# Bucket features of an LSH attention on one 64-row block a head instead of four 32-row blocks, with score steps of two PSUM banks

## The chip, the cores and the metric

The kernel runs on one core of a Trainium2 chip. The metric is the device time of one execution in microseconds. A run of several executions gives a median with the lowest and the highest; beside it one execution is recorded by the hardware profiler, and all views of the profile are of that one.

## What is computed

The reference is an attention with locality-sensitive buckets, followed by a gated MLP. Cut to what matters here:

```
q_bucket = bits of (q @ proj > 0)          # 6 bits a row
k_bucket = bits of (k @ proj > 0)
mask   = q_bucket == k_bucket
scores = where(mask, q @ k.T / sqrt(D), -1e9)
attn   = exp(scores - max) / (sum + 1e-9)
x      = attn @ v                          # 4 batches, 8 heads, 768 rows, head size 64
h      = gelu(x @ w_in)                    # then split into u and v
out    = x + (u * (w_sg @ norm(v) + b_sg)) @ w_out
```

All values are float32. The kernel gets the precision with split operands: each matrix is held as a high and a low part, and a product is a sum of three matmuls (high x high, low x high, high x low).

## The kernel before, in words

The kernel has an attention stage and then an MLP stage. The change edits the attention stage.

**Head pairs.** The 32 heads are taken as 16 pairs (`NPAIR`). The two heads of a pair lie one above the other: head 0 on rows (partitions) 0 to 63, head 1 on rows 64 to 127. `parts` transposes q and k on TensorE (L476) and splits them into a high part (L480, ScalarE) and a low part (L483, VectorE). A score matmul then reads 64 rows, and the two heads' matmuls stand beside each other in the array.

**Bucket features.** The mask is not applied afterwards but added inside the score matmul. `features` projects q and k with a signed copy of `proj` (L498) and turns the signs into feature rows (L501): 12 rows a block, six bits each with both signs, and one row in front of them (`MROW` = 0) which holds, on the q side, the shift (the negated maximum of the row) and ones on the k side. So one matmul over 13 rows adds both a huge negative number where the buckets differ and the shift. `block(b)` is the slice of these 13 rows: it starts at row `b * BL` and is `1 + 2 * NB` = 13 rows long. In the kernel before, `BL` is 32: there are four blocks, at rows 0, 32, 64 and 96, two with the same content for each head (head j has blocks 2j and 2j + 1).

**A score step.** There are 96 steps, six for each pair. `maxima(g + AHEAD)` runs `largest` for one tile of 128 query rows, five steps ahead, and `weigh` handles two tiles of 128 keys (`two`) against 384 queries.

- `largest` makes approximate scores with the features (L520) and the high parts (L523), for two halves `kh` of the keys and two heads `j`: four results of 128x384, each in a PSUM bank of its own. VectorE reduces each to its row maximum (L531). Group 0 issues all four 13-row matmuls and then the two 64-row matmuls of half 0; group 1 issues the two of half 1.
- After three tiles, `shift` combines the maxima (L543, L544), lays them out over the blocks with an identity matmul (L550), and ScalarE copies one row for each block into the features of q (L556, four copies).
- `weigh` makes the exact scores of both key tiles: group 0 issues all four 13-row matmuls (L574), then the three passes of the first key tile (L579, two heads each); group 1 issues the three passes of the second. ScalarE takes the exponentials (L586). `product` multiplies them with v (L592; eight matmuls of 128 rows and 64 columns), and the exponentials are added up for the denominators (L601) by the engine that `ADDS` names for the key tile: GpSimd for all five.
- `finish` sums over the partitions with matmuls (L617) and divides.

**What sets the order.** The order of all instructions is written out ahead by `Plan.order`. Every group of instructions is added with an engine, an estimated cost, a priority, and the buffers that it reads and writes. The planner simulates the engines and takes, for each engine, the group that can start first, and among those that can start then the one with the lowest priority number; a group with a better priority that could start within `SOON` times the cost is waited for. Step g has priority 2g for `weigh` (+ 0.01 for its second group), 2g + `S0P` for its `largest`, 2g + `AVP` for the product; `PREP`, `SHIFTP`, `FINP`, `WSTEP` and `WP` are the offsets of the preparation of a pair, the shift, the finish and the splitting of the MLP's weights. `form` marks groups of another tile shape, for which the planner adds 0.09. PSUM has eight banks: one holds the product (`NAV` = 1), the other seven are given out by `ps_tile` to whatever group asks; a group starts only when all of its banks are free. Group 0 of `weigh` and group 0 of `largest` ask for four each, since the features of both halves are written there.

Of the kernel before, what the change touches and what calls it, by code (L numbers as in the profile page):

```python
# [15 lines left out]
ALU = mybir.AluOpType  # L16
# [4 lines left out]

MLP = {"xl": "POOL", "gm": "DVE", "gl": "POOL", "wg": 398.29, "wo": 46.93, "x": 568.79}

AVP = 3.77
NAV = 1
S0P = 0.84
AHEAD = 5
PREP, SHIFTP, FINP, WSTEP, WP = -0.26, 2.36, 2.39, 13, 13.23
LOADS = "SP"
ADDS = ["POOL", "POOL", "POOL", "POOL", "POOL"]  # L30


class Plan:
# [3 lines left out]


    WAIT = 0.18
    SOON = 0.32  # L40
    TICK, WARM = 3.413, 0.49
    TURN_PE = 0.09
    LANES = 8
# [58 lines left out]
    def order(self):  # L102
# [32 lines left out]
        while len(out) < len(G):  # L135
# [10 lines left out]
            def early(n):  # L146
                e = G[n]["e"]
                return not wants[n] or e not in first or first[e] == n
# [5 lines left out]
            g = G[n]  # L154
            soon = [m for m in ready[e] if early(m) and max(when(m), since(m)) <= t0 + self.SOON * g["c"] and (G[m]["p"], m) < (g["p"], n)]
            if soon:
# [62 lines left out]
def kernel(  # L219
# [16 lines left out]
    nc = tc.nc  # L236

    B, H, S, D = q.shape
    P = 128
    NT = S // P  # L240
    HT = NT // 2
    SH = S // 2
# [6 lines left out]
    NB = proj.shape[1]  # L249
# [4 lines left out]
    EMPTY = 2.0 ** 32  # L254
# [20 lines left out]

    BL, MROW = 32, 0
    pr = const.tile([P, NB], F32, name="pr")
    for j in range(2):  # L280
        nc.scalar.dma_start(pr[j * D:(j + 1) * D], proj)
# [3 lines left out]
    for s in range(2):  # L285
        pv = pw[:, s, :].rearrange("p (b c) -> p b c", c=BL)
        for j in range(2):
            for r in range(2):
                c0 = 1 + NB * r
                nc.vector.tensor_scalar_mul(pv[j * D:(j + 1) * D, 2 * j:2 * j + 2, c0:c0 + NB],  # L290
                                            pr[j * D:(j + 1) * D].unsqueeze(1).to_broadcast([D, 2, NB]),
                                            1.0 if r == s else -1.0)
    pwh = const.tile([P, 2, P], F32R, name="pwh")
    pwl = const.tile([P, 2, P], F32R, name="pwl")
    nc.scalar.copy(pwh, pw)
# [7 lines left out]
    for s in range(2):  # L303
        for r in range(2):
            c0 = 1 + NB * r
# [60 lines left out]
    PE, DVE, ACT, POOL, SP = "PE", "DVE", "ACT", "POOL", "SP"  # L366
    xs = [[dram.tile([P, S], F32, name=f"xs_{b}_{hp}") for hp in range(NP)] for b in range(B)]

    plan = Plan()
# [45 lines left out]
    if True:  # L415
# [27 lines left out]
        def block(b):  # L443
            return slice(b * BL, b * BL + 1 + 2 * NB)

        def row(j):
            return slice(j * D, (j + 1) * D)
# [59 lines left out]
        def largest(st, t, prio):  # L507

            hf, i = divmod(t, HT)
            if i == 0:  # L510
                st.mx = late.ring([P, 2, HT, 2], F32, "mx", 3)
            mx, qs = st.mx, slice(t * P, (t + 1) * P)
            sc = [[ps_tile() for j in range(2)] for kh in range(2)]

            def mm(kh):
                if kh == 0:
                    for h in range(2):
                        for j in range(2):
                            b = block(2 * j + h)
                            nc.tensor.matmul(sc[h][j]()[:, :SH], st.ft[0]()[b, qs], st.ft[1]()[b, h * SH:(h + 1) * SH],  # L520
                                             start=True, stop=False)
                for j in range(2):
                    nc.tensor.matmul(sc[kh][j]()[:, :SH], st.hi[0]()[row(j), qs], st.hi[1]()[row(j), kh * SH:(kh + 1) * SH],  # L523
                                     start=False, stop=True)

            for kh in range(2):
                plan.add(PE, (0.36, 0.18)[kh], prio + 0.01 * kh, lambda kh=kh: mm(kh),
                         [(st.hi[0], hf), (st.hi[1], kh)] + ([(st.ft[0], hf), st.ft[1]] if kh == 0 else []),
                         sc[kh] + (sc[1] if kh == 0 else []), form="row")
                for j in range(2):  # L530
                    plan.add(DVE, 0.56, prio, lambda j=j, kh=kh: nc.vector.tensor_reduce(  # L531
                        mx()[:, kh, i, j:j + 1], sc[kh][j]()[:, :SH], axis=AX.X, op=ALU.max, negate=True),
                        [sc[kh][j]], [(mx, (kh, j, i))])

        def shift(st, hf, prio):

            mx, m, tp = st.mx, plan.buf("m", len(msts), lambda i: msts[i % len(msts)]), ps_tile()
            V = nc.vector

            def twice():  # L540
                return mx()[:, 0].rearrange("p i j -> p (i j)").unsqueeze(2).to_broadcast([P, 2 * HT, 2])

            plan.add(DVE, 0.16, prio, lambda: V.tensor_tensor(mx()[:, 0], mx()[:, 0], mx()[:, 1], op=ALU.min), [mx], [mx], port=True)  # L543
            plan.add(DVE, 0.16, prio, lambda: V.scalar_tensor_tensor(  # L544
                m()[:, :, MROW::BL].rearrange("p i (j a) -> p (i j) a", a=2), twice(), EMPTY, twice(), op0=ALU.is_lt, op1=ALU.mult),
                     [mx], [m], port=True)

            def spread():
                for i in range(HT):
                    nc.tensor.matmul(tp()[:, i * P:(i + 1) * P], m()[:, i, :], identr, start=True, stop=True)  # L550

            plan.add(PE, 0.35, prio, spread, [m], [tp])
            ft, cs = st.ft[0], slice(hf * SH, (hf + 1) * SH)
            for b in range(4):
                r = b * BL + MROW
                plan.add(ACT, 0.47, prio, lambda r=r: nc.scalar.copy(ft()[r:r + 1, cs], tp()[r:r + 1, :SH]), [tp], [(ft, hf)])  # L556

        def weigh(st, hf, k0, prio):

            cs, two = slice(hf * SH, (hf + 1) * SH), (k0, k0 + 1)  # L560
            if k0 == 0:
                st.av = ps_t.ring([P, 512], F32, "av", NAV)
                st.sum = [late.ring([P, SH], F32, "sum", 4) for _ in range(2)]
            av, sums = st.av, st.sum
            sc, p = [[ps_tile() for j in range(2)] for _ in two], [[p_tile() for j in range(2)] for _ in two]
            (qh, kh), (ql, kl), (qf, kf) = st.hi, st.lo, st.ft

            def mm(i):
                if i == 0:

                    for a, kt in enumerate(two):
                        for j in range(2):
                            b = block(2 * j + a)
                            nc.tensor.matmul(sc[a][j]()[:, :SH], kf()[b, kt * P:(kt + 1) * P], qf()[b, cs],  # L574
                                             start=True, stop=False)
                ks = slice(two[i] * P, (two[i] + 1) * P)
                for n, (x, y) in enumerate(((kh, qh), (kl, qh), (kh, ql))):
                    for j in range(2):
                        nc.tensor.matmul(sc[i][j]()[:, :SH], x()[row(j), ks], y()[row(j), cs], start=False, stop=(n == 2))  # L579

            for i, kt in enumerate(two):
                plan.add(PE, (0.72, 0.53)[i], prio + 0.01 * i, lambda i=i: mm(i),
                         [(x, hf) for x in (qh, ql)] + [(x, kt // HT) for x in (kh, kl)] + ([(qf, hf), kf] if i == 0 else []),
                         sc[i] + (sc[1] if i == 0 else []), form="row")
                for j in range(2):
                    plan.add(ACT, 0.5, prio, lambda i=i, j=j: nc.scalar.activation(p[i][j]()[:, :SH], sc[i][j]()[:, :SH], AF.Exp),  # L586
                             [sc[i][j]], [p[i][j]])

            def product():
                for i, kt in enumerate(two):  # L590
                    for j in range(2):
                        nc.tensor.matmul(av()[row(j), :SH + 1], st.v()[:, j, kt, :], p[i][j](), start=(kt == 0), stop=(kt == NT - 1))  # L592

            plan.add(PE, 1.48, prio + AVP, product, p[0] + p[1] + [st.v], [av], form="col")
            for i, kt in enumerate(two):
                if kt == 0:
                    continue
                e = ADDS[kt - 1]
                for j in range(2):
                    def add(j=j, i=i, first=p[0][j] if kt == 1 else sums[j]):  # L600
                        (nc.gpsimd if e == POOL else nc.vector).tensor_add(sums[j](), first()[:, :SH], p[i][j]()[:, :SH])  # L601

                    plan.add(e, 1.01 if e == POOL else 0.55, prio + 0.6, add, [p[i][j]] + ([p[0][j]] if kt == 1 else []),
                             [sums[j]], port=True)
# [51 lines left out]
        def maxima(i):  # L656
            n, t = divmod(i, NT)
            if n >= NPAIR:
                return
            p0 = 2 * (i - AHEAD) + S0P  # L660
            largest(sts[n], t, p0)
# [8 lines left out]
        for n in range(NPAIR):  # L670
            for c in range(NT):
                if c == 0:
                    prepare(n + 1)
                hf, k0, g = c // HT, 2 * (c % HT), NT * n + c
# [196 lines left out]
    for b in range(B):  # L871
        p = 500 + 1000 * b
        h = hidden(b, xx, p)
# [40 lines left out]
```

## Time and profile before

| | us |
|---|---|
| median of 3 runs | 870.92 |
| lowest, highest | 868.95, 871.54 |
| the profiled execution | 871.28 |
| its span in the trace | 869.5 |
| the attention's score steps, first to last score matmul | 27.2 to 511.2 |

In the profile PE is TensorE, PEld its weight loads, DVE VectorE, ACT ScalarE, POOL GpSimd and SP the engine that issues the transfers. A row of a group names the line, the engine, the operation, what it writes and reads, the shapes as partitions x elements, and the count; then come the busy time in us and the mean length of one in ns, and then the idle time of the engine just ahead of the group's instructions with what ended it. In a row of the timeline the first number is the start, the second the length of the merged piece, and L12 is line 12 of the kernel. Matmuls are pipelined, so the length of one is longer than the distance to the next, and the distance between starts says what a matmul costs when others follow. `g` is one of the seven shared PSUM tiles, `fq` and `fk` are the features, `hq`, `hk` the high parts, `lq`, `lk` the low parts, `p` the exponentials and `av` the product with v.

### The profile page before, as it was taken

The page shows a single profiled execution, that of the slowest core. Times are in us where ns is not written, and L with a number is a line of the kernel's source. Part 1 is how long each engine was busy: PE and PEld are TensorE (multiplying, and loading weights), DVE is VectorE, ACT ScalarE, POOL GpSimd, SP SyncE. Part 2 cuts the span into 40 slices and gives each one's busy share as a digit, 9 for nine tenths or more (in the row PEclk, how much of TensorE's full clock was granted, in tenths as well). Part 3 has the DMA queues.
Part 4 walks back from the last instruction along what each step waited for, and adds up shares of the span by engine and source line. Part 5 has one row for each costly group of instructions (what it writes and reads, how often), then busy time and mean ns, then how long its engine had stood idle before and what let it go on. Part 6 is the DMA issues. An engine that isn't in the chain of part 4 may idle for free.

```text
span 869.5 us, 15645 instructions
## 1 busy us (share of the span) xinstructions
PE 837.3 (96%) x5480; PEld 600.6 (69%) x5480; DVE 572.3 (66%) x1241; ACT 447.4 (51%) x990; POOL 443.9 (51%) x470
## 2 busy tenths in 40 slices
PE   7999999999999999999999979879889999999998
PEld 5655565565565555566656537879788989988996
DVE  7957876777776787687777515988972419515830
ACT  2556666666656656666666754542433225423511
POOL 0567768677767766867777793134111501510030
PEclk9889999999999999999999998979989999999999
DMA  5121321232132132133221123330013240122003
GB/s 139 43 56 50 95 79 53 79 96 65 59 87 74 50 95 67 49 96 93 58 61 53 58 68 111 136 95 27 25 37 124 70 145 1 37 73 74 1 1 121
DMA packets 100590, 60.86 MB, mean 70 GB/s; under 512 B 65696, under 2 KB 92320, under 8 KB 100512
## 3 DMA queue, kind: packets, MB, share of 16 engines
q1 hardware_dynamic: 99200, 56.85, 23.3%
q10 hardware_dynamic: 1312, 3.02, 1.0%
q8 instruction: 43, 0.70, 0.4%
q14 instruction: 35, 0.29, 0.1%
HBM read 47.06 MB, written 12.68 MB: 69 GB/s over the span
## 4 chain that ended last, share of the span: by engine, by line
PE 83%; DVE 8%; DMA 5%; issue 1%; ACT 1%; SPq 1%; POOL 0%; DVEq 0%; ACTq 0%
PE av L592 15%; PE g L579 13%; PE ps_vs L831 11%; PE ps_o L857 8%; PE g L520 6%; PE ps_h L813 6%; PE g L523 6%; PE ps_h L784 4%; PE g L498 4%; PE g L574 4%; PE g L476 3%; PE g L550 2%; PE g L617 2%; PE ps_o L862 1%; DMA rs<-r 1%
## 5 line engine op out<-in xcount | busy, mean ns | idle before, releaser
L601 POOL TENSOR_TENSOR sum<-sum,p 128x384 f32<-128x384 f32 x256 | 255.0, 1030 | 62.4 <-ACT p L586 62.4
L531 DVE TENSOR_REDUCE mx<-g 128x1 f32<-128x384 f32 x384 | 187.0, 549 | 95.7 <-PE g L523 95.6
L586 ACT ACTIVATE p<-g 128x384 f32<-128x384 f32 x384 | 157.6, 494 | 77.5 <-PE g L579 77.4
L592 PE MATMUL av<-p,v 128*64 128x385 f32 x768 | 146.5, 503 | 0.0
L592 PEld LDWEIGHTS av<-p,v 128*64 128x64 f32 x768 | 46.9, 137 | 52.5 <-issue 49.9
L601 POOL TENSOR_TENSOR sum<-p,p 128x384 f32<-128x384 f32 x64 | 63.6, 1015 | 33.2 <-ACT p L586 31.5
L579 PE MATMUL g<-hq,hk 64*128 64x384 f32 x384 | 76.0, 392 | 0.0
L769 DVE SCALAR_TENSOR_TENSOR h<-h,ps_h 128x384 f32<-128x384 f32 (+1 forms) x56 | 33.2, 605 | 64.8 <-ACT h L768 64.4
L794 POOL TENSOR_TENSOR mv<-mv,epsr 128x1 f32<-128x1 f32 x24 | 13.2, 551 | 111.8 <-DVE mv L793 106.6
L556 ACT CAST fq<-g 1x384 fp32r<-1x384 f32 x128 | 60.2, 470 | 13.5 <-PE g L550 12.3
L831 PE MATMUL ps_vs<-wgh,zh 128*128 128x384 f32 x192 | 65.4, 341 | 0.1
L857 PE MATMUL ps_o<-woh,gs 128*128 128x512 f32 x192 | 65.5, 402 | 0.0
L579 PE MATMUL g<-lq,hk 64*128 64x384 f32 x384 | 65.4, 336 | 0.0
L579 PE MATMUL g<-hq,lk 64*128 64x384 f32 x384 | 65.3, 336 | 0.0
L831 PE MATMUL ps_vs<-wgl,zh 128*128 128x384 f32 x192 | 64.9, 338 | 0.0
L831 PE MATMUL ps_vs<-wgh,zl 128*128 128x384 f32 x192 | 64.8, 338 | 0.0
L842 POOL TENSOR_TENSOR gs<-gt,gs 128x384 fp32r<-128x384 f32 x32 | 32.5, 1018 | 60.4 <-ACT gs L839 60.4
L639 POOL TENSOR_TENSOR xt<-xt,e 128x384 f32<-128x384 f32 x32 | 32.5, 1015 | 59.6 <-ACT e L637 49.9
L520 PE MATMUL g<-fk,fq 13*128 13x384 f32 x384 | 61.6, 444 | 0.3
L523 PE MATMUL g<-hk,hq 64*128 64x384 f32 x384 | 60.3, 393 | 0.0
L520 PEld LDWEIGHTS g<-fk,fq 13*128 13x128 f32 x384 | 34.4, 184 | 27.9 <-issue 13.9
L813 PE MATMUL ps_h<-xh,wih 128*128 128x384 f32 x128 | 45.2, 353 | 8.5 <-DVE y L773 7.9
(126 smaller groups left out, 1674.1 us busy)
## 6 DMA issues: line engine op xcount, KB each, us to landing
q<-in_q_dram SPq DMA_DIRECT2D x32, 192.0 KB, 3.0
k<-in_k_dram SPq DMA_DIRECT2D x32, 192.0 KB, 3.4
v<-in_v_dram SPq DMA_DIRECT2D x16, 384.0 KB, 3.4
rs<-r SPq DMA_DIRECT2D x64, 96.0 KB, 2.8
xs<-xt SPq DMA_DIRECT2D x32, 192.0 KB, 2.0
x<-xs SPq DMA_DIRECT2D x16, 384.0 KB, 3.2
rx<-xs SPq DMA_DIRECT2D x96, 64.0 KB, 2.0
out_dram<-ob SPq DMA_DIRECT2D x24, 256.0 KB, 2.1
```

Of the source, the lines that this page charges most:

```text
L498: nc.tensor.matmul(fp()[:, :SH], w[:, s, :], x()[:, cs], start=(i == 0), stop=(i == 2))
L520: nc.tensor.matmul(sc[h][j]()[:, :SH], st.ft[0]()[b, qs], st.ft[1]()[b, h * SH:(h + 1) * SH], start=True, stop=False)
L523: nc.tensor.matmul(sc[kh][j]()[:, :SH], st.hi[0]()[row(j), qs], st.hi[1]()[row(j), kh * SH:(kh + 1) * SH], start=False, stop=True)
L531: plan.add(DVE, 0.56, prio, lambda j=j, kh=kh: nc.vector.tensor_reduce(mx()[:, kh, i, j:j + 1], sc[kh][j]()[:, :SH], axis=AX.X, op=ALU.max ...
L556: plan.add(ACT, 0.47, prio, lambda r=r: nc.scalar.copy(ft()[r:r + 1, cs], tp()[r:r + 1, :SH]), [tp], [(ft, hf)])
L579: nc.tensor.matmul(sc[i][j]()[:, :SH], x()[row(j), ks], y()[row(j), cs], start=False, stop=(n == 2))
L586: plan.add(ACT, 0.5, prio, lambda i=i, j=j: nc.scalar.activation(p[i][j]()[:, :SH], sc[i][j]()[:, :SH], AF.Exp), [sc[i][j]], [p[i][j]])
L592: nc.tensor.matmul(av()[row(j), :SH + 1], st.v()[:, j, kt, :], p[i][j](), start=(kt == 0), stop=(kt == NT - 1))
L601: (nc.gpsimd if e == POOL else nc.vector).tensor_add(sums[j](), first()[:, :SH], p[i][j]()[:, :SH])
L813: nc.tensor.matmul(ps()[:, :SH], w[:, c, fs], x()[:, cs], start=(c == 0 and n == 0), stop=(c == NC - 1 and n == 2))
L831: nc.tensor.matmul(vp(), z()[:, t, fs], w()[:, t, cs], start=(t == 0 and n == 0), stop=(t == NT - 1 and n == 2))
L857: nc.tensor.matmul(po(), a()[:, ts_], w()[:, f, :], start=(f == 0 and n == 0), stop=False)
```

## The change

`BL` goes from 32 to 64, so there is one block of 13 feature rows for each head, at rows 0 and 64. The blocks' 13-row slice itself, `block(b)`, is as before. `largest` and `weigh` are written as two groups each that ask for two banks: each group of `largest` issues the two 13-row matmuls of its half and then the two 64-row ones; each group of `weigh` issues the three passes of its key tile and then the two 13-row matmuls. `shift` writes two rows instead of four and ScalarE copies two. The planner's costs follow, the priorities' offsets get other values, and the addition for the fourth key tile goes from GpSimd to VectorE.

```diff
-AVP = 3.77
+AVP = 1.5
 NAV = 1
-S0P = 0.84
+S0P = 1.0
 AHEAD = 5
-PREP, SHIFTP, FINP, WSTEP, WP = -0.26, 2.36, 2.39, 13, 13.23
+PREP, SHIFTP, FINP, WSTEP, WP = -1, 2, 2.7, 12, 8
 LOADS = "SP"
-ADDS = ["POOL", "POOL", "POOL", "POOL", "POOL"]
+ADDS = ["POOL", "POOL", "DVE", "POOL", "POOL"]
...
-    SOON = 0.32
+    SOON = 0.2
...
-    BL, MROW = 32, 0
+    BL, MROW = 64, 0
...
-                nc.vector.tensor_scalar_mul(pv[j * D:(j + 1) * D, 2 * j:2 * j + 2, c0:c0 + NB],
-                                            pr[j * D:(j + 1) * D].unsqueeze(1).to_broadcast([D, 2, NB]),
-                                            1.0 if r == s else -1.0)
+                nc.vector.tensor_scalar_mul(pv[j * D:(j + 1) * D, j, c0:c0 + NB], pr[j * D:(j + 1) * D], 1.0 if r == s else -1.0)
...
             def mm(kh):
-                if kh == 0:
-                    for h in range(2):
-                        for j in range(2):
-                            b = block(2 * j + h)
-                            nc.tensor.matmul(sc[h][j]()[:, :SH], st.ft[0]()[b, qs], st.ft[1]()[b, h * SH:(h + 1) * SH],
-                                             start=True, stop=False)
-                for j in range(2):
-                    nc.tensor.matmul(sc[kh][j]()[:, :SH], st.hi[0]()[row(j), qs], st.hi[1]()[row(j), kh * SH:(kh + 1) * SH],
-                                     start=False, stop=True)
+                for n, x in enumerate((st.ft, st.hi)):
+                    for j in range(2):
+                        r = (block, row)[n](j)
+                        nc.tensor.matmul(sc[kh][j]()[:, :SH], x[0]()[r, qs], x[1]()[r, kh * SH:(kh + 1) * SH],
+                                         start=(n == 0), stop=(n == 1))
 
             for kh in range(2):
-                plan.add(PE, (0.36, 0.18)[kh], prio + 0.01 * kh, lambda kh=kh: mm(kh),
-                         [(st.hi[0], hf), (st.hi[1], kh)] + ([(st.ft[0], hf), st.ft[1]] if kh == 0 else []),
-                         sc[kh] + (sc[1] if kh == 0 else []), form="row")
+                plan.add(PE, 0.36, prio + 0.01 * kh, lambda kh=kh: mm(kh),
+                         [(st.hi[0], hf), (st.hi[1], kh), (st.ft[0], hf), (st.ft[1], kh)], sc[kh], form="row")
...
-                m()[:, :, MROW::BL].rearrange("p i (j a) -> p (i j) a", a=2), twice(), EMPTY, twice(), op0=ALU.is_lt, op1=ALU.mult),
+                m()[:, :, MROW::BL], mx()[:, 0], EMPTY, mx()[:, 0], op0=ALU.is_lt, op1=ALU.mult),
...
-            for b in range(4):
+            for b in range(2):
...
             def mm(i):
-                if i == 0:
-
-                    for a, kt in enumerate(two):
-                        for j in range(2):
-                            b = block(2 * j + a)
-                            nc.tensor.matmul(sc[a][j]()[:, :SH], kf()[b, kt * P:(kt + 1) * P], qf()[b, cs],
-                                             start=True, stop=False)
                 ks = slice(two[i] * P, (two[i] + 1) * P)
-                for n, (x, y) in enumerate(((kh, qh), (kl, qh), (kh, ql))):
+                for n, (x, y) in enumerate(((kh, qh), (kl, qh), (kh, ql), (kf, qf))):
                     for j in range(2):
-                        nc.tensor.matmul(sc[i][j]()[:, :SH], x()[row(j), ks], y()[row(j), cs], start=False, stop=(n == 2))
+                        r = block(j) if n == 3 else row(j)
+                        nc.tensor.matmul(sc[i][j]()[:, :SH], x()[r, ks], y()[r, cs], start=(n == 0), stop=(n == 3))
 
             for i, kt in enumerate(two):
-                plan.add(PE, (0.72, 0.53)[i], prio + 0.01 * i, lambda i=i: mm(i),
-                         [(x, hf) for x in (qh, ql)] + [(x, kt // HT) for x in (kh, kl)] + ([(qf, hf), kf] if i == 0 else []),
-                         sc[i] + (sc[1] if i == 0 else []), form="row")
+                plan.add(PE, 0.71, prio + 0.01 * i, lambda i=i: mm(i),
+                         [(x, hf) for x in (qh, ql, qf)] + [(x, kt // HT) for x in (kh, kl, kf)], sc[i], form="row")
```

More of the change, by code (lines that the diff above doesn't have):

```diff
@@ L538, in shift @@
             V = nc.vector
-            def twice():
-                return mx()[:, 0].rearrange("p i j -> p (i j)").unsqueeze(2).to_broadcast([P, 2 * HT, 2])
             plan.add(DVE, 0.16, prio, lambda: V.tensor_tensor(mx()[:, 0], mx()[:, 0], mx()[:, 1], op=ALU.min), [mx], [mx], port=True)
             plan.add(DVE, 0.16, prio, lambda: V.scalar_tensor_tensor(
-                m()[:, :, MROW::BL].rearrange("p i (j a) -> p (i j) a", a=2), twice(), EMPTY, twice(), op0=ALU.is_lt, op1=ALU.mult),
+                m()[:, :, MROW::BL], mx()[:, 0], EMPTY, mx()[:, 0], op0=ALU.is_lt, op1=ALU.mult),
                      [mx], [m], port=True)
```

## The prediction

> **What bounds the kernel now.** I read the page's busy shares first, then its slices with the granted clock, then the busy time of the engines in the attention stage (from the first to the last score matmul), and then TensorE's timeline, step by step.
>
> ```profile
> PE   837.3 (96%) x5480; PEld 600.6 (69%) x5480; DVE 572.3 (66%) x1241; ACT 447.4 (51%) x990; POOL 443.9 (51%) x470
> ...
> PE   7999999999999999999999979879889999999998
> ...
> PEclk9889999999999999999999998979989999999999
> ...
> 27.20:511.20 484.00, 480.07 (x3699) 284.29 (x3695) 349.19 (x739) 309.26 (x732) 350.42 (x357) 0.99 0.26 69
> ```
>
> The last row is the attention stage; its columns after the length are the busy times of PE, PEld, DVE, ACT and POOL, the granted clock, and DMA. PE works 480 of 484 us at a granted clock of 0.99, while DVE and POOL have some 134 us free each. The change edits this stage alone. The stage has 96 score steps (16 head pairs of six), so one takes 484 / 96 = 5.04 us, and the kernel's time follows PE's time per step. What lies outside the stage runs the same instructions before and after; I leave it as it is.
>
> Busy time says nothing about what a matmul costs when they overlap. For that I take the starts of the next view: one whole step of the timeline without side work, from one `weigh` to the next (columns: start, length, engine, line).
>
> ```profile
> 256.09 0.45 PE L574 MATMUL g<-fq,fk 13*128 13x384 f32 x4
> 256.47 0.45 PE L579 MATMUL g<-hq,hk 64*128 64x384 f32 x2
> 256.75 0.34 PE L579 MATMUL g<-hq,lk 64*128 64x384 f32 x2
> 256.93 0.34 PE L579 MATMUL g<-lq,hk 64*128 64x384 f32 x2
> 257.11 0.34 PE L579 MATMUL g<-hq,hk 64*128 64x384 f32 x2
> 257.29 0.34 PE L579 MATMUL g<-hq,lk 64*128 64x384 f32 x2
> 257.46 0.34 PE L579 MATMUL g<-lq,hk 64*128 64x384 f32 x2
> 257.74 0.61 PE L520 MATMUL g<-fk,fq 13*128 13x384 f32 x4
> 258.28 0.61 PE L523 MATMUL g<-hk,hq 64*128 64x384 f32 x4
> 258.82 1.51 PE L592 MATMUL av<-p,v 128*64 128x385 f32 x8
> 260.26 0.44 PE L574 MATMUL g<-fq,fk 13*128 13x384 f32 x4
> ```
>
> I call a set of matmuls that run side by side a slot, and a change of form a place where the next slot has another tile shape. Three prices come out of the starts.
>
> - A slot followed by its own kind: from 256.75 to 257.46 there are four, 0.71 / 4 = 0.178 us each. A slot is two 64-row matmuls here. The four 13-row matmuls of L574 are also one slot: together they last 0.45 us, about as long as one pair.
> - The last slot before a change: 257.74 - 257.46 = 0.28, so 0.10 more.
> - The first slot after a change: 256.75 - 256.47 = 0.28, again 0.10 more.
>
> A change of form thus costs 0.20 us, half on each side of it. The lone slot of L574, with a change on both sides, should then take 0.178 + 0.20 = 0.38; it takes 256.47 - 256.09 = 0.38. The same can be seen over the whole run in the mean lengths of the groups:
>
> ```profile
> L579 PE MATMUL g<-hq,hk 64*128 64x384 f32 x384 | 76.0, 392 | 0.0
> L579 PE MATMUL g<-lq,hk 64*128 64x384 f32 x384 | 65.4, 336 | 0.0
> L520 PE MATMUL g<-fk,fq 13*128 13x384 f32 x384 | 61.6, 444 | 0.3
> L574 PE MATMUL g<-fq,fk 13*128 13x384 f32 x384 | 43.9, 442 | 0.6 <-DVE mx L531 0.6
> L523 PE MATMUL g<-hk,hq 64*128 64x384 f32 x384 | 60.3, 393 | 0.0
> ```
>
> Matmuls that never stand first after a change last 336 ns (lq,hk). The 13-row ones, which always do, last 442 to 444, 0.106 more. Those that do half of the time (hq,hk, and L523) lie in between, at 392 and 393. So the price holds for all 384, and it is paid between 13-row and 64-row tiles as between any others.
>
> One more thing is in L520: it has as many matmuls as L574 but 61.6 us of busy time against 43.9. In the step above its four took 0.61 us instead of 0.45: the last of the four starts late, since the step asks for four free PSUM banks at once. That wait is 17.7 / 96 = 0.18 us a step.
>
> Sum of the score part of the step as it is: 10 slots (1 + 6 in `weigh`, 1 + 2 in `largest`) x 0.178 = 1.78; changes: in, three inside, out; the outer two count half, so 4 x 0.20 = 0.80; the bank wait 0.16 here. That is 2.74, and the timeline has 258.82 - 256.09 = 2.73. The model closes.
>
> **The change part by part.** *Slots.* With one block a head, only the two heads of one key tile go side by side, not two heads by two key tiles. `weigh` goes from 7 slots to 8, `largest` from 3 to 4: 2 x 0.178 = +0.36 us a step.
>
> *Changes of form.* The slice that the matmuls read is still 1 + 2 x 6 = 13 rows, so I take their tile to stay the 32-row one, now at rows 0 and 64. Each `weigh` half becomes three 64-row slots and one 13-row slot; each `largest` half one 13-row and one 64-row slot. With all four halves in a row (S 64 rows, F 13 rows): SSSF SSSF FS FS. That has six changes inside against three now (FSSSSSS FSS). With the P·V product L592 between the two `weigh` halves, as the planner may well place it now that the halves are separate and AVP is 1.5, the change from F to S there is swallowed by the two that the product has in any case, and the first `weigh` half joins the last `largest` half as S to S: two more changes instead of three. Strict alternation of the halves (SSSF FS SSSF FS) leaves one more. I expect the first two orders in about equal numbers, since side work (transposes, projections) decides in each step whether the product is ready: 2.5 x 0.20 = +0.50 us a step.
>
> The Trainium skill, "TensorEngine Tiling (Array Packing)", section Key Properties, says that changing the tiling mode, not just the tile, drains TensorE; this speaks against the change. The trace agrees on the 0.10 us before a change (257.46 to 257.74), but shows as much again behind it (256.47 to 256.75), which a drain alone does not name. By the drain alone the added changes would come to 2.5 x 0.10 x 96 = 24 us instead of 48; the rows decide for 48.
>
> *Banks.* Two banks a step instead of four, of seven: the late fourth matmul should go, -0.18 us a step. What remains late next is PE itself, so the gain is real; if the wait only moves, it is lost.
>
> *Other engines.* The two rows of the shift in place of four take 64 copies off ACT, and one addition in five goes from POOL to DVE (the last two rows are from the view of waits: who waited for whom, us in total, times, longest):
>
> ```profile
> L556 ACT CAST fq<-g 1x384 fp32r<-1x384 f32 x128 | 60.2, 470 | 13.5 <-PE g L550 12.3
> L601 POOL TENSOR_TENSOR sum<-sum,p 128x384 f32<-128x384 f32 x256 | 255.0, 1030 | 62.4 <-ACT p L586 62.4
> L531 DVE TENSOR_REDUCE mx<-g 128x1 f32<-128x384 f32 x384 | 187.0, 549 | 95.7 <-PE g L523 95.6
> PE g L617 <- POOL sum L601: 5.4, 2, 5.0
> PE g L617 <- ACT p L586: 2.7, 3, 1.1
> ```
>
> ACT loses 64 x 0.47 = 30 us of 309, POOL 64 x 1.03 = 66 of 350, neither of which PE waits for except the 8 us at L617 (the sums), of which up to 5 may go. DVE gains 64 additions. It does none of this shape now; between its reduction of a 128x384 tile (0.549) and POOL's addition (1.03) that is 35 to 66 us, and I take 35, the same engine and size. It lies beside DVE's 135 us of idle time, and the stage gets longer. Queued behind a DVE addition are the reductions that free the banks of `largest`; if every addition held up PE by its length, 35 us would come on top, but with two banks a step there are three spare ones, so I count nothing. The weight jobs and other planner numbers only move work within queues that are not full; no transfer is added or removed, and SP's and POOL's queues issue the same. Zero for these.
>
> Sum: 0.36 + 0.50 - 0.18 = +0.68 us a step, x 96 = +65 us. The profiled execution took 871.28 us (span 869.5), 0.4 over the median of 870.92. That gives 871.3 + 65 = 936 us.
>
> **The rivals.** *The 13-row matmuls take the 64-row form.* If the two blocks at rows 0 and 64 run in the form of the score passes, no change is left inside the step: 0.36 - 3 x 0.20 - 0.18 = -0.42 us a step, -41 us, 830 us: faster. It decides at the first S to F of a step, which would then be 0.178 instead of 0.28. DVE would have 349 + 35 = 384 us in 443, so the gain could be had. For it: the 64-row spacing of the blocks, and that the row positions are the same as those of the passes. Against it: the 13-row matmuls in the trace of before stand at rows 0 and 64 too, together with 32 and 96, and pay the full price against 64-row ones.
>
> *The order alternates.* One more change only: 0.36 + 0.20 - 0.18 = 0.38 a step, 36 us, 908 us; with the 5 us of L617, 902. For it: each half is now its own group of two banks. Against it: priorities put both `weigh` halves ahead of `largest` (2g against 2g + 1).
>
> *The bank wait stays* while the halves stand in a row: 0.36 + 0.60 = 0.96 a step, 92 us, 963 us. For it: the seven banks are the same, and `weigh` and `largest` of a step ask for eight. Against it: they no longer ask for four at once, and consumers get more time per step.
>
> **How the numbers follow.** The forecast (two or three more changes, wait gone: 926 to 946 us) gets 0.62; alternating order 0.12; bank wait 0.12; the 64-row form 0.11; 0.03 is left for effects that cancel nearly. The range must hold 0.8: from 902 to 962 it takes in the first three (0.86) and leaves out the 830. About 0.3% is what a measurement of this kernel tells from no change (the runs shown span 868.95 to 871.54). Faster by more than that is the 64-row form, 0.11; within it 0.02; slower the rest, 0.87.
>
> **What would show it.** The 13-row matmuls stay 768 in all, but stand in the timeline as slots of two (three slots of L579 and one of two 13-row matmuls in each `weigh` half) in place of fours. Their mean length shows the form: near 0.34 us if they run as the score passes do, 0.40 to 0.44 if they change form; and in the latter case the mean of the 64-row group behind them (hq,hk) stays near 0.39 and that of L523's rises towards 0.44. A step should take some 5.7 us in place of 5.04, with PE busy nearly all of the stage and the granted clock unchanged, and the late start inside the 13-row slots of `largest` should be gone. The order of the halves shows which count of changes holds. The prediction is wrong if a 64-row slot follows a 13-row one after 0.18 us, or if PE is seen waiting for DVE or ACT inside the steps.

## The result, and the profile after

The change makes the kernel slower: 949.41 us median of four runs (944.45 to 952.64) against 870.51 of four, a ratio of 1.0903 (95% interval 1.0851 to 1.0955). The profiled execution took 944.45 us, its span is 942.7, so 73.2 us more than the span of before. The prediction was 936 us, with 902 to 962.

From the page of the kernel after, the rows that answer to the first fence of the prediction. The last row is the busy time of the engines over its attention stage, here from the first `weigh` to the MLP's first matmul.

```profile
PE 916.1 (97%) x5480; PEld 615.7 (65%) x5480; DVE 620.5 (66%) x1369; ACT 419.5 (45%) x926; POOL 316.7 (34%) x342
...
PEclk8999999998999999999998999998999999999999
...
28.00:596.20 568.20, 565.67 (x3717) 304.96 (x3717) 394.66 (x868) 285.49 (x676) 232.05 (x239) 0.98 0.22 60
```

The row of before for the same stretch:

```profile
28.00:520.40 492.40, 483.06 (x3715) 284.91 (x3715) 349.25 (x740) 312.01 (x738) 359.62 (x367) 0.99 0.26 69
```

PE has the same 5480 matmuls in the whole run and works 565.67 of 568.2 us in this stretch. It is still the bound, and the stage is longer: the MLP's first matmul starts at 596.5 us instead of 520.9. What follows takes 346 us against 349. All of the loss lies in the attention stage. From the first to the last score matmul, as the prediction took the stage, it is some 562 us (28.1 to 590.5) instead of 484: 5.86 us a step, where 5.7 was forecast.

The timeline of one step after, from product to product (start, length, engine, line):

```profile
247.73 1.51 PE L574 MATMUL av<-p,v 128*64 128x385 f32 x8
249.18 0.45 PE L562 MATMUL g<-hq,hk 64*128 64x384 f32 x2
249.46 0.34 PE L562 MATMUL g<-hq,lk 64*128 64x384 f32 x2
249.63 0.34 PE L562 MATMUL g<-lq,hk 64*128 64x384 f32 x2
249.90 0.45 PE L562 MATMUL g<-fq,fk 13*128 13x384 f32 x2
250.28 0.44 PE L562 MATMUL g<-hq,hk 64*128 64x384 f32 x2
250.56 0.34 PE L562 MATMUL g<-hq,lk 64*128 64x384 f32 x2
250.73 0.33 PE L562 MATMUL g<-lq,hk 64*128 64x384 f32 x2
250.99 0.44 PE L562 MATMUL g<-fq,fk 13*128 13x384 f32 x2
251.86 0.55 PE L539 MATMUL g<-identr,m 128*128 128x128 f32 x3 [0.43 <-DVE m L533]
252.34 0.44 PE L517 MATMUL g<-fk,fq 13*128 13x384 f32 x2
252.71 0.44 PE L517 MATMUL g<-hk,hq 64*128 64x384 f32 x2
253.08 0.44 PE L517 MATMUL g<-fk,fq 13*128 13x384 f32 x2
253.45 0.44 PE L517 MATMUL g<-hk,hq 64*128 64x384 f32 x2
253.82 1.51 PE L574 MATMUL av<-p,v 128*64 128x385 f32 x8
```

The prices are those of before. A slot after its own kind is 249.63 - 249.46 = 0.17; the last before a change 249.90 - 249.63 = 0.27; a lone slot between two changes, be it 13 rows (250.28 - 249.90) or 64 rows (253.08 - 252.71), 0.37 to 0.38. In `largest` all four slots are such lone slots. The groups say it for the whole run:

```profile
L517 PE MATMUL g<-hk,hq 64*128 64x384 f32 x384 | 86.2, 445 | 0.0
L562 PE MATMUL g<-fq,fk 13*128 13x384 f32 x384 | 84.5, 436 | 0.0
L562 PE MATMUL g<-hq,hk 64*128 64x384 f32 x384 | 83.6, 431 | 0.0
L517 PE MATMUL g<-fk,fq 13*128 13x384 f32 x384 | 81.3, 417 | 0.0
L562 PE MATMUL g<-lq,hk 64*128 64x384 f32 x384 | 65.6, 336 | 0.0
```

The 64-row group of `largest`, 393 ns before, now has 445, the length of a first slot after a change. Most of the 13-row ones have it too: nearly all in `weigh` (436) and some three in four in `largest` (417), where the others follow the features of `weigh`. The program's order has 892 changes of form in the attention stage, against 590 before, and 1152 score slots against 960.

One thing is new. The granted clock drops in the middle of the stage. The busy times of three neighbouring stretches (PE's is the first number after the length, the granted clock the first number after the five engines):

```profile
211.47:214.89 3.42, 3.42 (x23) 2.00 (x23) 3.28 (x12) 2.95 (x7) 0.00 (x0) 1.00 0.26 78
214.89:218.30 3.41, 3.41 (x14) 1.31 (x10) 2.85 (x7) 0.02 (x1) 0.61 (x1) 0.50 0.11 33
218.30:221.71 3.41, 3.41 (x28) 1.99 (x26) 1.19 (x3) 1.75 (x4) 2.26 (x3) 1.00 0.09 32
```

For one stretch of 3.41 us the clock is half, though PE was busy all through the stretch ahead of it. The trace has eight of these between 200 and 550 us (from 214.9, 232.0, 269.5, 433.3, 450.4, 501.6, 508.4 and 546.0); before had none between 49 and 519 us. Each costs half its length: 8 x 1.7 = 13.6 us. What stood in the stretch ahead of the first of them:

```profile
211.59 0.44 PE L562 MATMUL g<-hq,hk 64*128 64x384 f32 x2
211.87 0.34 PE L562 MATMUL g<-hq,lk 64*128 64x384 f32 x2
212.04 0.34 PE L562 MATMUL g<-lq,hk 64*128 64x384 f32 x2
212.31 0.44 PE L562 MATMUL g<-fq,fk 13*128 13x384 f32 x2
212.67 0.55 PE L539 MATMUL g<-identr,m 128*128 128x128 f32 x3
213.15 0.44 PE L517 MATMUL g<-fk,fq 13*128 13x384 f32 x2
213.52 0.44 PE L517 MATMUL g<-hk,hq 64*128 64x384 f32 x2
213.89 0.44 PE L517 MATMUL g<-fk,fq 13*128 13x384 f32 x2
214.26 0.44 PE L517 MATMUL g<-hk,hq 64*128 64x384 f32 x2
214.64 2.63 PE L574 MATMUL av<-p,v 128*64 128x385 f32 x8
```

Seven changes of form between these slots (S is a 64-row slot, F a 13-row one): S to F, F to the shift, from it to F, then F S F S and the product, which begins at 214.64. Between 49 and 580 us all eight slow stretches follow one with seven changes; 12 others with seven, and all 134 with another number (two with eight, the rest with fewer), are followed by full clock. The Trainium skill, "TensorE: Matmul & The Clock Gate", Part 1, says that the clock is set to half or full by how busy PE was in windows of 3.413 us; the trace agrees on the length and the half. Its rule there, no PE idle gaps of more than about 3.4 us, does not cover this case, since the profile shows no gap here. That the time inside the changes counts as missing activity is my reading; no run shows it by itself.

### The profile page after: what moved, and what is told of

Its sections match the earlier page's. It is cut to its first block, busy times and chain, and to the rows that moved or that the text cites. A ratio compares the mean times of both kernels' runs of the same rounds, so it can differ in the third digit from the quotient of the medians.

```text
span 942.7 us, 15438 instructions
## 1 busy us (share of the span) xinstructions
PE 916.1 (97%) x5480; PEld 615.7 (65%) x5480; DVE 620.5 (66%) x1369; ACT 419.5 (45%) x926; POOL 316.7 (34%) x342
## 4 chain that ended last, share of the span: by engine, by line
PE 83%; DVE 9%; DMA 4%; issue 1%; SPq 1%; ACT 1%; POOL 0%; ACTq 0%; DVEq 0%
PE g L562 21%; PE av L574 15%; PE g L517 14%; PE ps_vs L813 8%; PE ps_o L839 7%; PE ps_h L795 5%; PE ps_h L766 4%; PE g L496 3%; PE g L474 3%; PE g L539 2%; PE g L599 1%; DMA rs<-r 1%; PE ps_o L844 1%; DMA q<-in_q_dram 1%; DVE owx L353 1%
## 5 line engine op out<-in xcount | busy, mean ns | idle before, releaser
L568 ACT ACTIVATE p<-g 128x384 f32<-128x384 f32 x384 | 168.1, 487 | 221.4 <-PE g L562 217.6
L583 POOL TENSOR_TENSOR sum<-sum,p 128x384 f32<-128x384 f32 x128 | 126.9, 1017 | 193.8 <-ACT p L568 180.8
L574 PE MATMUL av<-p,v 128*64 128x385 f32 x768 | 154.9, 527 | 0.0
L517 PE MATMUL g<-hk,hq 64*128 64x384 f32 x384 | 86.2, 445 | 0.0
L562 PE MATMUL g<-fq,fk 13*128 13x384 f32 x384 | 84.5, 436 | 0.0
L583 DVE TENSOR_TENSOR sum<-sum,p 128x384 f32<-128x384 f32 x128 | 68.8, 561 | 19.8 <-ACT p L568 15.5
L517 PE MATMUL g<-fk,fq 13*128 13x384 f32 x384 | 81.3, 417 | 0.0
L562 PEld LDWEIGHTS g<-hq,hk 64*128 64x128 f32 x384 | 36.7, 187 | 64.7 <-issue 49.4
L562 PEld LDWEIGHTS g<-fq,fk 13*128 13x128 f32 x384 | 35.4, 181 | 48.6 <-issue 48.6
L517 PEld LDWEIGHTS g<-hk,hq 64*128 64x128 f32 x384 | 36.3, 186 | 39.5 <-issue 39.5
```

The costliest lines, as they stand in the source:

```text
L517: nc.tensor.matmul(sc[kh][j]()[:, :SH], x[0]()[r, qs], x[1]()[r, kh * SH:(kh + 1) * SH], start=(n == 0), stop=(n == 1))
L562: nc.tensor.matmul(sc[i][j]()[:, :SH], x()[r, ks], y()[r, cs], start=(n == 0), stop=(n == 3))
```

## The experiments

Times are medians, each beside runs of the kernel before on the same chip, which had 867.4 to 869.6. "After" means 949.4, or 944.45 where the profiled executions are compared; it was not run again, and the kernel before had 870.5 beside it, so chips differ by some 3 us at most.

**Features that read 64 rows, so that no change is left between slots of the scores.** The other rows of a block hold zeros.

```diff
 def block(b):
-    return slice(b * BL, b * BL + 1 + 2 * NB)
+    return slice(b * BL, (b + 1) * BL)
```

> The kernel after, with one edit: the feature matmuls read the whole block of 64 rows instead of its first 13 (the other rows hold zeros), so their tile has the shape of the score passes. Slots stay, form changes in the attention stage fall from 892 to 361 as the program's order counts them. Theory (a form change costs 0.20 us, a slot 0.178): 531 x 0.20 = 106 us less than after, and none of the eight stretches of half clock (13.6 us): about 825 us; reckoned from the kernel before (192 more slots, 229 fewer changes, no bank wait) 842 us. So 825 to 845, faster than both kernels. Rival (the time comes from the 192 more slots and the planner's order): 945 us, no different from after.

Measured 863.51 us; against before 0.9934 (0.9911 to 0.9956). That is 86 us under after with the same number of matmuls and the same planner numbers: the rival, that slots and order make the loss, falls. The lowest expectation of 825 us was not reached. The group rows of this kernel:

```profile
L562 PE MATMUL g<-fq,fk 64*128 64x384 f32 x384 | 71.4, 334 | 0.0
L517 PE MATMUL g<-hk,hq 64*128 64x384 f32 x384 | 73.5, 343 | 0.0
```

The same feature matmul of `weigh` that took 436 ns in after takes 334, and the 64-row one of `largest`, which stands behind features, 343 instead of 445. No slow stretch is left in the stage before 515.1 us, 0.9 us ahead of the MLP's first matmul. Its busy times by half show where it could be faster still, and the two longest of PE's waits in the stage say for whom it waited (us in total, times, longest):

```profile
30.00:270.00 240.00, 226.63 (x1788) 147.80 (x1786) 228.50 (x475) 135.11 (x328) 119.75 (x121) 1.00 0.27 75
270.00:480.00 210.00, 207.91 (x1658) 137.25 (x1650) 164.84 (x354) 119.94 (x293) 94.59 (x98) 1.00 0.23 63
```

```profile
PE g L474 <- DVE mx L524: 4.2, 6, 0.7
PE g L562 <- ACT p L568: 3.8, 10, 0.8
```

In the first half DVE (third engine) is busy 228.5 of 240 us and PE only 226.6: PE is no longer the only bound there. Its waits for DVE and ACT in the stage come to some 15 us, all but 0.9 of it before 300 us.

**The same in one place alone.** First `weigh`, then `largest`:

```diff
-                        r = block(j) if n == 3 else row(j)
+                        r = row(j)
```

> The kernel after with 64-row features in weigh alone; largest keeps 13 rows. Form changes 684 against 892. Theory: 208 x 0.20 = 42 us less than after, and up to 13.6 us for stretches of half clock that go: 890 to 903 us. Rival (the time of after comes from the slots): 945 us.

```diff
-                        r = (block, row)[n](j)
+                        r = row(j)
```

> The kernel after with 64-row features in largest alone; weigh keeps 13 rows. Form changes 663 against 892. Theory: 229 x 0.20 = 46 us less than after, and up to 13.6 us for stretches of half clock that go: 890 to 903 us. Rival (what is gained in weigh alone, 47 us, was the whole of it): 940 us or more.

Measured 902.05 and 894.84 us. Both parts of the change lose by the same cause, and about the same: 47 us for 208 changes, 55 for 229. Two slow stretches and one are in the stage; unlike those of after, each follows a wait of PE for DVE (0.8, 0.6 and 0.6 us).

**The same matmuls, put back to back.** The second half of `weigh` puts its features ahead of its passes, and the first half of `largest` behind them, so that features meet features. Shape and count of every matmul stay.

```diff
-                for n, x in enumerate((st.ft, st.hi)):
+                for n, x in enumerate(((st.hi, st.ft), (st.ft, st.hi))[kh]):
...
-                for n, (x, y) in enumerate(((kh, qh), (kl, qh), (kh, ql), (kf, qf))):
+                ps = ((kh, qh), (kl, qh), (kh, ql))
+                for n, (x, y) in enumerate(((*ps, (kf, qf)), ((kf, qf), *ps))[i]):
...
```

> The kernel after, with the feature matmuls of neighbouring groups put back to back: the second half of weigh and the first half of largest change the order of their own passes, nothing else. Form changes fall from 892 to 745, slots stay. Theory: 147 x 0.20 = 29 us less, and with fewer changes close together some or all of the half-clock stretches gone (up to 13.6 us): 902 to 916 us. Rival (a slot of two 13-row matmuls is slow by itself, wherever it stands): 945 us as after.

Measured 907.57 us, within the range of the theory, and no slow stretch is left inside the stage. Two feature slots that stand together:

```profile
243.79 0.34 PE L563 MATMUL g<-lq,hk 64*128 64x384 f32 x2
244.06 0.62 PE L563 MATMUL g<-fq,fk 13*128 13x384 f32 x4
244.61 0.44 PE L563 MATMUL g<-hq,hk 64*128 64x384 f32 x2
```

They take 244.61 - 244.06 = 0.55 us, which is two slots of 0.178 and one change of 0.20. A slot of two 13-row matmuls isn't slow by itself. This is the cleanest test of the price, since nothing but the order of passes differs. From the profiled executions (944.45 and 908.24), less 13.6 us of clock, 22.6 us remain for 147 changes: 0.15 us each. The two runs before it give 0.16 in the same way: (944.45 - 901.50 - 10.2) / 208 and (944.45 - 895.23 - 11.9) / 229. The starts in the timeline say 0.20, in these kernels too; the difference is some 7 to 9 us a kernel. A part of it is waiting that came in place of changes: PE waits 4.0, 6.9 and 4.6 us for DVE and POOL in the stages of these three (in the order back to back, `weigh` alone, `largest` alone), and 2.5 in that of after. The rest stays open.

**One part of the change in the kernel before.** `largest` in two groups of two banks, with four blocks as before.

```diff
-                if kh == 0:
-                    for h in range(2):
-                        for j in range(2):
-                            b = block(2 * j + h)
+                for j in range(2):
+                    b = block(2 * j + kh)
...
-                         sc[kh] + (sc[1] if kh == 0 else []), form="row")
+                         sc[kh], form="row")
```

> The kernel before with one part of the change: largest works in two groups of two banks, each with the two 13-row matmuls of its half ahead of its two 64-row ones; still four blocks of 32 rows, weigh and the planner numbers as before. Form changes 781 against 590, 96 more slots. Theory: 191 x 0.20 = 38 for changes, 96 x 0.178 = 17 for slots, 18 less for the bank wait that goes: 37 us more, 905 us. Rival (two banks a step gain more than the changes cost): 870 us or less. If the bank wait stays: 922 us.

Measured 920.89 us, near the third figure; but the bank wait is not what stayed: the timeline has no 13-row slot of `largest` whose matmuls start apart any more. The last matmul of the attention starts 41.7 us later than in before. The theory has 37 for it, and the clock adds 8.5: 34.1 us at half clock up to there (17.6 to 44.9 and 376.0 to 382.8 us) against 17.1 in before. The two together are 4 us too many. Another 9 us are lost at the hand-over to the MLP, whose first matmul waits for x (first row; the second is a wait 19 us later, for `y`, a result of the MLP itself):

```profile
PE ps_h L781 <- ACT xh L715: 9.2, 1, 9.2
PE ps_h L781 <- DVE y L770: 4.1, 1, 4.1
```

**The planner's numbers by themselves.** The new numbers in the kernel before, and the old ones in the kernel after:

```diff
-AVP = 3.77
+AVP = 1.5
-S0P = 0.84
+S0P = 1.0
-PREP, SHIFTP, FINP, WSTEP, WP = -0.26, 2.36, 2.39, 13, 13.23
+PREP, SHIFTP, FINP, WSTEP, WP = -1, 2, 2.7, 12, 8
-ADDS = ["POOL", "POOL", "POOL", "POOL", "POOL"]
+ADDS = ["POOL", "POOL", "DVE", "POOL", "POOL"]
-    SOON = 0.32
+    SOON = 0.2
```

> The kernel before with the planner numbers of the kernel after (offsets, SOON, additions on VectorE), blocks and passes as before. Form changes 611 against 590. Theory: 21 x 0.20 = 4 us more, 875 us, give or take 5. Rival (the new planner numbers make the loss): over 900 us.

> The kernel after with the planner numbers of the kernel before (all additions back on GpSimd). Form changes 896 against 892. Theory: 945 us like after, give or take 6 (the half-clock stretches may fall otherwise). Rival (the new planner numbers make the loss): under 900 us.

Measured 895.82 us, 27 over before, and 956.4 us, 7 over after and outside its range: two misses, of which the first is the large one. So the numbers are no small matter in the kernel before, but are nothing that after loses by: with the old ones it has the same attention (last matmul 592.4 against 596.2 us) and then waits 8.8 us more at the hand-over. In the kernel before the new numbers bring the splitting of the MLP's weights forward: the last tile of `w_in` is done at 224 us instead of 479, and DVE is busy 210.81 of the 240 us from 30 to 270, where it was 179.66 in before. Then I asked whether the additions on DVE do it:

```diff
-ADDS = ["POOL", "POOL", "DVE", "POOL", "POOL"]
+ADDS = ["POOL", "POOL", "POOL", "POOL", "POOL"]
```

> As e3_before_new_numbers (the kernel before with the new planner numbers, 896 us), with only the additions put back on GpSimd. Form changes 575 against 611. Theory A (VectorE in the first half costs e3 its time): first eight pairs from 270 to some 250 us, 7 us less for changes: 868 to 876 us. Theory B (the offsets of the order cost it): 890 us.

> As e1_rows64, with only the additions put back on GpSimd; offsets new. Theory A: the first eight head pairs (254.8 us in e1_rows64) come down to the 30.0 us of the later ones, 15 us less: about 849 us. Theory B (VectorE in the first half is held by the weight splitting alone, or is not what counts): 860 us or more.

Measured 901.37 and 878.18 us: both are worse than with the additions on DVE, by 6 and 15 us. Theory A falls in both, and that it would get worse neither theory says. With the new offsets the additions on DVE aren't the cause. With the old offsets they do count:

```diff
-ADDS = ["POOL", "POOL", "POOL", "POOL", "POOL"]
+ADDS = ["POOL", "POOL", "DVE", "POOL", "POOL"]
```

> The kernel before with one number of the change: the fourth key tile's additions on VectorE, all offsets as before (form changes 587 against 590). Theory A (VectorE additions hold up the reductions when the steps are short): 875 to 885 us. Theory B (they lie beside the idle time of VectorE, as the prediction had it): 866 to 872 us.

Measured 881.55 us, 1.0141 of before (1.0102 to 1.0180). Additions on DVE cost 12 us where the steps are short. The offsets and `SOON` alone cost 34 (901.37 against 867.41 beside it), both together 27, so the two don't add up. Which of the offsets does it stays open.

**The 64-row features with the old numbers.** The edit below to the kernel after, together with the planner numbers of the kernel before (additions on GpSimd, weights spread out); and then the weights asked for a little earlier (WSTEP 11, WP 8).

```diff
-    return slice(b * BL, b * BL + 1 + 2 * NB)
+    return slice(b * BL, (b + 1) * BL)
```

> The kernel after with features that read 64 rows (as in e1_rows64), and with all planner numbers of the kernel before: additions on GpSimd, weight splitting spread over a longer time. Form changes 318. Theory A (in e1_rows64 the gain was held back in the first half by VectorE, which the new numbers load with additions and early weight splitting): against the kernel before 34 us more for slots, 272 x 0.20 = 54 less for changes, 18 less for the bank wait: about 833 us. Theory B (without the changes the PSUM banks and their readers are the limit in all of the stage, as the late halves of pairs in the second half of e1_rows64 suggest, 30.0 us a head pair against 30.7): about 858 us.

> As e5_rows64_old_numbers (850 us), with the weight splitting asked for earlier (WSTEP 11, WP 8), since in e5 the MLP stage's first matmuls wait for x while the last weight tiles are still being split. Theory: the 12 us of waits at the hand-over go: 838 to 842 us. Rival (the hand-over is set by the attention's last results alone): 850 us.

Measured 849.65 us, 0.9778 of before (0.9744 to 0.9812), the fastest of all, and 852.68 us. In the first, a head pair takes some 29 us against 30.7 in before, and the product's last group starts at 480.1 us instead of 512.8: 33 us of the 38 that theory A asks for. A third of it is given back behind that, 7 us at the hand-over, where the MLP's first matmul waits for x (first row), and 5 in the MLP, where a wait for its own `y` comes 20 us later (second row):

```profile
PE ps_h L766 <- ACT xh L700: 8.3, 1, 8.3
PE ps_h L766 <- DVE y L755: 4.5, 1, 4.5
```

Asking for the weights earlier took the wait for x away and lengthened the attention by 10 us, so that nothing was won: a miss. It does show that in the 64-row kernel the weights' offsets alone can cost the attention that much.

## Why the prediction was right, point by point

**The mechanism.** Right. The time is PE's time per step, and what was added to it is 192 slots and the changes of form between 32-row and 64-row tiles. Reading 64 rows instead of 13 takes the changes away and 86 us with them; putting the same matmuls in another order takes 42.

**Slots.** Right: 1152 against 960, 192 x 0.178 = 34 us.

**Changes.** The price in the timeline was right, the number too small. I took 2.5 more a step from two orders in equal shares; there are (892 - 590) / 96 = 3.15. The two orders did come, but not in equal shares: of the six steps of a pair, four have all four halves in a row and two have the product after the first half of `weigh`, which by the prediction's own counts is 2.67. The rest, 0.48 a step, is side work, which I left out. The shift L539 in the step shown (twice a pair) and one of the transposes L474 now stand between two slots of the scores and bring two changes where there would be one or none; in before they stood beside the product, where there is a change in any case. At 0.20 that is 60 us in place of 48: the term that was mis-sized. The group rows say the same: the 64-row group hq,hk of `weigh` has 431 ns, where I expected it to stay near 390, since nearly all of it now stands behind a change and not half.

**Banks.** Right: the late fourth matmul is gone, about 18 us. In after, the 13-row matmuls of L517 take 81.3 us for 192 slots, 0.42 each, which is no longer than their mean of 417 ns.

**Other engines.** Next to nothing on the path, as predicted (PE's waits for DVE inside the steps come to 0.6 us, one of them the 0.43 in the step shown), but with a wrong count. DVE got 128 additions, not 64:

```profile
L583 DVE TENSOR_TENSOR sum<-sum,p 128x384 f32<-128x384 f32 x128 | 68.8, 561 | 19.8 <-ACT p L568 15.5 <-POOL sum L583 4.2
```

The inner function `add` looks up `e` when it runs, after the loop over the two key tiles has ended, so the third key tile takes the engine of the fourth, while the planner has counted it for GpSimd. At 0.561 us each, as taken, they lie beside idle time in after, whose steps are long; in the kernel before they cost 12 us. The same holds for the planner numbers as a whole, which I put at zero: about true for after, where the old ones are 7 us slower, and 27 us in before. What the text named was the cover in after, and it did not say that the cover is made by the loss itself.

**The waits for sums.** 8.1 us before, 1.9 after; of the "up to 5" that I allowed for, 6 went.

**The clock.** I expected it unchanged. It fell, for 13.6 us in the profiled execution.

**The sum.** Slots 34, changes 60, bank wait -18, clock +14, sums -6, and -3 for a slow stretch of 6.8 us from 41.8 in before that after doesn't have: +81 us, where the MLP's first matmul came 75.6 us later. The 5 us too many have the sign and the size of the gap in the price of a change above; I did not trace them. The forecast of +65 left out 26 us, 12 by the number of changes and 14 by the clock. That it came within some 8 us of the profiled execution (936 against 944.45) is in part luck: what it also left out on the other side, 6 for the sums, 3 for the slow stretch of before, the 5 that are open and 2 behind the stage, takes most of that away.

**The rivals.** The 64-row form did not come about by the spacing of the blocks: the 13-row slots last 0.44 us. Its price of -41 us for the case that the form is met was too hopeful, too: with 64 rows read, 863.5 us with the new numbers and 849.7 with the old, not 830, since PE then waits for DVE and ACT in the first half (new numbers) or for x at the hand-over (old ones). The alternating order does not occur, and the bank wait did not stay. The range was said to hold the case of the bank wait, but its 963 us lie just outside the 962.

## What to carry to other kernels

The form of a small matmul is set by the rows it reads, not by where it stands: two matmuls of 13 rows cost a change of form on each side between passes of 64 rows, and reading 64 rows with zeros in them costs no more than any 64-row pass (334 ns against 336) and saves both. So before grouping small matmuls to have fewer of them, see whether they can take their neighbours' shape; and count changes of form in the program's order, which needs no run. The count ranks kernels as long as PE is what bounds them: the two kernels with 361 changes, which differ in the engine of the additions alone, are 15 us apart. A planner's offsets that were found with one bound are worth little with another: the same numbers were harmless in one kernel and cost 27 us in the other.

## What the runs showed of the hardware that I had not expected

A stage in which the profile shows PE busy without a gap can lose its clock: eight stretches of 3.41 us at half clock in the kernel after, four in the same kernel with the old planner numbers, with PE busy all through the 3.41 us ahead of each. In after all eight follow a stretch with seven changes of form; with the old numbers three follow one with six and one with seven, while 14 others with seven are followed by full clock. So the changes in the stretch ahead don't set it alone, and a rule that says which stretch it hits I don't have. With the changes moved together (745) or gone (361, new numbers) no such stretch is inside the stage. In all other kernels, every slow stretch that begins between 60 us and the last score matmul is another case: in the 3.41 us ahead of it PE waits 0.6 to 1.4 us, mostly for DVE (two such stretches with 684 changes, one with 663, one of double length with 781). Whether the spread of after, 944.45 to 952.64 us, comes from such stretches stays open: its slowest run has the lowest mean clock, 0.960, but the runs of 944.45 and 948.25 us both have 0.971.
